# Windowed attention and a gated feed-forward block: another load order and transposition for one group of tokens, and some of its work on ScalarE

## The chip, the cores and the metric

The kernel runs on one core of one Trainium2 chip. The metric is the device time of the program in microseconds (us), median of several runs. Four engines compute: TensorE (PE: matmuls, and transposes written as matmuls against an identity; PEld is its weight load), VectorE (DVE), ScalarE (ACT) and GpSimd (POOL). POOL and SyncE (SP) here issue transfers, which sixteen DMA engines carry out. Matmuls write to PSUM, eight banks that the program uses in turn; an engine has to copy ("evict") what is needed from there to the on-chip memory.

## The reference

Attention over a window of 128 tokens plus four "sink" tokens at the start, and then a gated feed-forward block on the joined heads:

```python
batch, n_heads, seq, head_dim = (4, 8, 768, 64)      # n_sink, window = (4, 128)
scores = scale * np.matmul(q, k.transpose(0, 1, 3, 2))
keep = is_sink | in_window
scores = np.where(keep, scores, -1000000000.0)
a = np.exp(scores - np.max(scores, axis=-1, keepdims=True))
a = a / (np.sum(a, axis=-1, keepdims=True) + 1e-09)
attn = np.matmul(a, v)
x = attn.transpose(0, 2, 1, 3).reshape(B * S, H * D)   # 3072 tokens x 512
g = x @ w_gate                                         # 512 x 1536
out = (g * (1.0 / (1.0 + np.exp(-g))) * (x @ w_val)) @ w_out
```

## The kernel before

The 3072 tokens are cut into twelve groups of 256, three to a batch. For each group, queries and keys are brought into a form with the head dimension on the partitions (`qT`, `kT`), scores are computed (`step_S`), exponentials taken, values summed and normalised (`step_PV`), and the result is transposed (`step_X`) into `xT`, the input of the feed-forward block. That block works through `gate` units (two projections, tanh, two passes on VectorE) and `down` units (the output weights). All engines' programs are written in one fixed order: `weave` runs the units one after another and puts attention steps of later groups into them by slot number, so that TensorE always has something to do.

Groups get their transposed queries and keys in three ways: group 0 from a special load; groups 1 and 2 from a load in *row order* (four tokens of a head to a partition, 1 KB runs in memory), followed by small matmuls; groups 3 to 11 from a load in *token order* (one token to a partition, all heads, 256-byte runs), followed by DMA transposes.

```python
rowp = pool("rowp", 3); natp = pool("natp", 2)      # buffers: three and two
...
def load_rows(g, pairs=ALL, tensors=(0, 1)):        # row order, four DMAs
    ...
            nc.gpsimd.dma_start(x[64 * w:64 * (w + 1), i, pairs],
                                by_rows((k, q)[i], b, w, pairs, c * 256))

def load_nat(g):                                    # token order, four DMAs
    x = natp.tile([P, 2, 2, DM], BF16, tag="nat", name="nat")
    for i, src in ((0, k), (1, q)):
        for j in range(2):
            ...
            nc.gpsimd.dma_start(x[:, i, j].rearrange("p (h d) -> p h d", d=D),
                                src[b, :, t0:t0 + P].rearrange("h p d -> p h d"))
...
# order of the loads on GpSimd's queue
load_rows(1); load_v(0); load_gate(0); load_gate(1, (0,)); load_v(1)
load_gate(1, (1,)); load_gate(2)
...
load_rows(2); load_gate(3); load_v(2); load_gate(4); load_gate(5)
for i in range(4):
    load_out(i)
...                                                 # the prologue's compute
load_nat(3); load_v(3)

def step_T(g, i, p2, evict=None):                   # from row order: 16 matmuls of 64 x 64
    pt = bank([P, 2, 256], FP32, "pt")
    for pp in range(2):
        for r in range(4):
            for w in range(2):
                h = slice(64 * w, 64 * (w + 1))
                nc.tensor.matmul(pt[h, pp, r:256:4], x[h, i, p, r * D:(r + 1) * D],
                                 ident[h, h], start=True, stop=True, ...)
    # one eviction: keys on ScalarE, queries on VectorE

def xbar(g):                                        # from token order: four DMA transposes
    for j in range(2):
        for i in range(2):
            nc.sync.dma_start_transpose((kTs, qTs)[i][b][:, :, t0:t0 + P], nats[g][:, i, j])

def step_PV(g, j, hh, norm="v"):                    # one half of the heads of 128 tokens
    ...                                             # matmuls into po
    def dve():
        nc.vector.reciprocal(rcp, po[:, :, D:D + 1])
        if norm == "a":                             # four scalings on ScalarE
            for hq in range(4):
                nc.scalar.activation(xn[:, hq], po[:, hq, 0:D], AF.Copy, scale=rcp[:, hq])
        else:                                       # one multiply on VectorE
            nc.vector.tensor_tensor(xn, po[:, :, 0:D], rcp.broadcast_to([P, 4, D]), op=ALU.mult)
    if norm == "a":
        dve()                                       # written at once
    else:
        later.append(dve)                           # written behind the unit's own passes

def step_X(g, j, evict="v"):                        # groups 0, 1, 2, 4: four transposes on TensorE
    ...                                             # others: a DMA transpose
    # "a": copy on ScalarE at once; "now": on VectorE at once; "v": on VectorE later

weave(us, slots(                                    # units 0-11 and 12-17: gates; 18-23: down
    (0, [K(1)]), (1, PVs(1)[:2] + [A(step_PV, 1, 0, 1, "a"), A(step_PV, 1, 1, 1, "a"), flush]),
    (2, [A(step_X, 1, 0, "a"), A(step_X, 1, 1, "a")]),
    ((4, 4, 5, 5), T(2)), ((6, 7), Ss(2)), (6, [K(2)]),
    ((8, 8, 9, 9), PVs(2)),
    ((10, 11), [A(step_X, 2, 0, "now"), A(step_X, 2, 1, "now")]),
    (11, [L(A(load_nat, 4), A(load_v, 4))]),
    (12, [A(xbar, 3)]), (12, [L(A(load_nat, 5), A(load_v, 5))]),
    (15, [A(xbar, 4)]), (15, [L(A(load_nat, 6), A(load_v, 6))]),
    ((17, 18), Ss(3)), ...
    ((19, 19, 19, 20), PVs(3)), (20, Xs(3)),
    ((19, 20), Ss(4)), (19, [K(4)]), ...
```

Of the kernel before, what the change touches and what calls it, by code (L numbers as in the profile page):

```python
# [7 lines left out]
FP32 = mybir.dt.float32  # L8
BF16 = mybir.dt.bfloat16
# [5 lines left out]
def kernel(  # L15
# [12 lines left out]
    nc = tc.nc  # L28
    P = 128
# [3 lines left out]
    DM = moe_w_gate.shape[0]  # L33
# [5 lines left out]
    NP2 = H // 2  # L39
    GC = S // 256  # L40
# [12 lines left out]
    def pool(name, bufs, psum=False):  # L53
        if psum:
            return ctx.enter_context(
                tc.tile_pool(name=name, bufs=bufs, space=bass.MemoryType.PSUM))
        return ctx.enter_context(tc.tile_pool(name=name, bufs=bufs))

    const = pool("const", 1)
    wpool = pool("wpool", 1)  # L60
    rowp = pool("rowp", 3)
    natp = pool("natp", 2)
# [15 lines left out]
    def bank(shape, dtype, name):  # L78
        return psum.tile(shape, dtype, tag="b", name=name)


    rows, nats, vas = {}, {}, {}

    def by_rows(src, b, w, pairs, t0):

        hs = slice(2 * pairs.start + w, 2 * pairs.stop, 2)
        return src[b, hs, t0:t0 + 256].rearrange("p (m r) d -> m p (r d)", r=4)

    ALL = slice(0, NP2)

    def new_rows(g):
        rows[g] = rowp.tile([P, 2, NP2, 4 * D], BF16, tag="rows", name="rows")
        return rows[g]

    def load_rows(g, pairs=ALL, tensors=(0, 1)):
        b, c = divmod(g, GC)
        x = rows[g] if g in rows else new_rows(g)
        for i in tensors:
            for w in range(2):
                nc.gpsimd.dma_start(  # L100
                    x[64 * w:64 * (w + 1), i, pairs],
                    by_rows((k, q)[i], b, w, pairs, c * 256))

    def load_nat(g):
        b, c = divmod(g, GC)
        x = natp.tile([P, 2, 2, DM], BF16, tag="nat", name="nat")
        for i, src in ((0, k), (1, q)):
            for j in range(2):
                t0 = c * 256 + j * P
                nc.gpsimd.dma_start(  # L110
                    x[:, i, j].rearrange("p (h d) -> p h d", d=D),
                    src[b, :, t0:t0 + P].rearrange("h p d -> p h d"))
        nats[g] = x

    def load_v(g):
        b, c = divmod(g, GC)
        va = vpool.tile([P, 2, H, VS], BF16, tag=f"va{g}", name="va")
        nc.vector.memset(va[:, :, :, D:D + 1], 1.0)
        for j in range(2):
            t0 = c * 256 + j * P  # L120
            nc.gpsimd.dma_start(  # L121
                va[:, j, :, 0:D], v[b, :, t0:t0 + P].rearrange("h p d -> p h d"))
        vas[g] = va
# [3 lines left out]
    def load_gate(i, which=(0, 1)):  # L127
        f0, n = sum(FCH[:i]) * P, FCH[i] * P
        both = (wgs, moe_w_gate, "wg"), (wvs, moe_w_val, "wv")
        for lst, w, nm in (both[x] for x in which):  # L130
            t = wpool.tile([P, DMC, n], BF16, tag=f"{nm}{i}", name=nm)
            nc.gpsimd.dma_start(  # L132
                t, w[:, f0:f0 + n].rearrange("(c p) f -> p c f", p=P))
            lst.append(t)

    def load_out(i):
        n = DFC // 4
        t = wpool.tile([P, n, DM], BF16, tag=f"wo{i}", name="wo")
        nc.gpsimd.dma_start(
            t, moe_w_out[i * n * P:(i + 1) * n * P].rearrange("(c p) f -> p c f", p=P))  # L140
        wos.append(t)

    ident = const.tile([P, P], BF16)
# [6 lines left out]
    th8 = const.tile([P, 4, 4], FP32)  # L150
    lt8 = const.tile([P, 4, 4], FP32)
    sk = const.tile([P, 1], FP32)
    zero = const.tile([P, 512], BF16)
    one = const.tile([P, 1], FP32)
    warmed = const.tile([P, 1], FP32)
    KW = 32
    kss = const.tile([P, B, NP2, KW + 2 * NS], BF16)
    vsbs = []

    nc.vector.memset(one, 1.0)  # L160
    nc.vector.memset(zero, 0.0)
    nc.vector.memset(vcf, 0.0)
    nc.vector.memset(vcf[:, :, D:D + 1], 1.0)
    nc.vector.memset(kss, 0.0)
# [22 lines left out]
    for i in range(2):  # L187
        nc.gpsimd.dma_start(x0[:, i, 4:8], by_two((k, q)[i], 4))  # L188
    load_rows(1)
    load_v(0)  # L190
    load_gate(0)
# [2 lines left out]
    load_gate(1, (1,))  # L194
    load_gate(2)
    nc.gpsimd.tensor_copy(out=vcf[64:128], in_=vcf[0:64])
    load_rows(2)
    load_gate(3)
    load_v(2)
    load_gate(4)  # L200
    load_gate(5)
    for i in range(4):
        load_out(i)

# [14 lines left out]
    kTs, qTs, es_t, e_t, xns, xTs = {}, {}, {}, {}, {}, {}  # L219
    later = []  # L220

    def flush():
        for f in later:
            f()
        later.clear()

    def new_T(b):
        if b not in kTs:
            kTs[b] = kqtp.tile([P, NP2, S], BF16, tag="kT", name="kT")
            qTs[b] = kqtp.tile([P, NP2, S], BF16, tag="qT", name="qT")  # L230

    def step_T(g, i, p2, evict=None):
        b, c = divmod(g, GC)
        new_T(b)
        x = rows[g]
        pt = bank([P, 2, 256], FP32, "pt")
        for pp in range(2):
            p = 2 * p2 + pp
# [3 lines that stand above are left out]
                    nc.tensor.matmul(  # L242
                        pt[h, pp, r:256:4], x[h, i, p, r * D:(r + 1) * D],
                        ident[h, h], start=True, stop=True, skip_group_check=True)
        dst = (kTs, qTs)[i][b][:, 2 * p2:2 * p2 + 2, c * 256:(c + 1) * 256]
        if (evict or ("a", "v")[i]) == "a":
            nc.scalar.copy(out=dst, in_=pt)
        else:
            nc.vector.tensor_copy(out=dst, in_=pt)

    def xbar(g):
        b, c = divmod(g, GC)
        new_T(b)
        for j in range(2):
            for i in range(2):
                t0 = c * 256 + j * P
                nc.sync.dma_start_transpose(  # L257
                    (kTs, qTs)[i][b][:, :, t0:t0 + P], nats[g][:, i, j])
# [210 lines left out]
    def A(fn, *a):  # L469
        return lambda: fn(*a)  # L470

    def T(g):
        return [A(step_T, g, i, p2) for p2 in range(2) for i in range(2)]

    def Ss(g):
        return [A(step_S, g, p2) for p2 in range(2)]

    def PVs(g):
        return [A(step_PV, g, j, hh) for hh in range(2) for j in range(2)]
# [4 lines left out]
    def K(g):  # L484
        return A(step_K, g)
# [18 lines left out]
        return sl  # L504


    def fill(n, ps, cols=512):
        for _ in range(n):
            nc.tensor.matmul(ps[:, 0:cols], zero[:, 0:P], zero[:, 0:cols], start=True,
                             stop=True, skip_group_check=True)  # L510
# [23 lines left out]
    def pair_S(p, n=0):  # L534
        if p == 0:
            e_t[0] = epool.tile([P, H, 512], BF16, tag="e", name="e")
        pss = [bank([P, 512], FP32, "s") for _ in range(2)]
        fill(n, pss[0], 256)
        for kk, n, col in ((0, 256, P), (P, P, 3 * P)):
            for h in range(2):  # L540
                r = slice(h * D, (h + 1) * D)
                nc.tensor.matmul(
                    pss[h][:, col:col + n], kTs[0][r, p, kk:kk + P],
                    qTs[0][r, p, kk:kk + n], start=True, stop=True)
        for h in range(2):
            nc.scalar.activation(
                e_t[0][:, 2 * p + h, P:512], pss[h][:, P:512], AF.Exp, scale=scale)

    def pair_mask(p):
        e = e_t[0][:, 2 * p:2 * p + 2, P:512]  # L550
        m = mask0.rearrange("q (o a) x -> q o (a x)", o=1)[:, :, P:512]
        nc.vector.tensor_tensor(e, e, m.broadcast_to([P, 2, 384]), op=ALU.mult)

    fill(8, bank([P, 512], FP32, "w"))
    for i, p in ((0, 0), (1, 0), (0, 1), (1, 1)):
        cast(i, p)
    pair_T(0)
    pair_T(1)
    pair_S(0, 1)
    pair_S(1)  # L560
    pair_T(2)
    pair_T(3)
# [3 lines left out]
    for p in range(1, NP2):  # L566
        pair_mask(p)
    step_T(1, 0, 0, "a")
    step_T(1, 0, 1, "a")
    step_T(1, 1, 0, "a")  # L570
    step_T(1, 1, 1, "a")
# [12 lines left out]
    step_S(1, 1)  # L584
    later[:0] = masks1
    flush()
    load_nat(3)
    load_v(3)

    g0, g1, g2 = gates(0), gates(1), gates(2)  # L590
    us = [g0[0], g0[1], g0[2], g1[0], g1[1],
# [3 lines left out]
    def L(*fs):  # L595
        def f():
            for x in fs:
                x()
        return f

    weave(us, slots(
        (0, [K(1)]), (1, PVs(1)[:2] + [A(step_PV, 1, 0, 1, "a"), A(step_PV, 1, 1, 1, "a"), flush]),
        (2, [A(step_X, 1, 0, "a"), A(step_X, 1, 1, "a")]),
        ((4, 4, 5, 5), T(2)), ((6, 7), Ss(2)), (6, [K(2)]),
        ((8, 8, 9, 9), PVs(2)),
        ((10, 11), [A(step_X, 2, 0, "now"), A(step_X, 2, 1, "now")]),
        (11, [L(A(load_nat, 4), A(load_v, 4))]),
        (12, [A(xbar, 3)]), (12, [L(A(load_nat, 5), A(load_v, 5))]),
        (15, [A(xbar, 4)]), (15, [L(A(load_nat, 6), A(load_v, 6))]),
        ((17, 18), Ss(3)), (18, [A(step_ks, 1)]), (18, [A(step_vsb, 1)]),  # L610
        (17, [A(xbar, 5)]), (17, [L(A(load_nat, 7), A(load_v, 7))]),
# [60 lines left out]
```

The softmax here doesn't subtract the row's maximum and nothing guards it: scores larger than these inputs give would overflow.

## Time and profile before

| | before |
|---|---|
| time, median of 3 runs | 242.69 us (242.56 to 242.87) |
| span of the profiled execution | 240.2 us |
| TensorE busy | 230.8 us, 96% |
| VectorE busy | 159.6 us, 66% |
| ScalarE busy | 110.6 us, 46% |
| read from and written to the chip's large memory | 28.34 MB, 6.29 MB |

The profile is of one execution. Its page gives each engine's busy time; the span in forty slices of 6 us, one digit each in tenths; the DMA queues (q0 is the one that GpSimd feeds; q1 carries what SyncE issues, DMA transposes and output stores); the chain of work that ended last; and groups of equal instructions. A timeline lists instructions in order of time with equal ones merged: start, length, engine, line, operation, output<-inputs, shape, count, and in brackets the idle time before and what ended it. Matmuls overlap in the pipeline, so a matmul's printed length is longer than the time for which it holds TensorE.

### The profile page before, as it was taken

The numbers are of one execution on the slowest core, as the hardware profiler recorded it, in microseconds if no ns is written. First come the engines' busy times: TensorE is split into PE (matmuls) and PEld (weight loads), VectorE is DVE, ScalarE is ACT, GpSimd is POOL, SyncE is SP. The second block draws the span as 40 slices with busy tenths as digits, with TensorE's granted clock in tenths as the row PEclk, the third lists the DMA queues.
The fourth block names the chain that finished last, engine by engine and source line by source line (L and its number), as shares of the span: only waits on it lengthen the run. The fifth ranks groups of instructions, "written<-read, shape, count | busy, mean of one in ns | idle before, by whom it ended". The sixth has DMA issues, their size and how long they took to land.

```text
span 240.2 us, 5002 instructions
## 1 busy us (share of the span) xinstructions
PE 230.8 (96%) x1951; PEld 131.9 (55%) x1975; DVE 159.6 (66%) x340; ACT 110.6 (46%) x223; POOL 72.1 (30%) x94
## 2 busy tenths in 40 slices
PE   7999999997999999999999999999999999999994
PEld 3667877884545444454445444445444445488443
DVE  5698589886653698970597981488971498877000
ACT  4896474235541755511756612556611662232112
POOL 8976764705926209700082600000000000000000
PEclk9999999999999999999999999999999999999999
DMA  7999999999999999995699957550207200200132
GB/s 132 165 185 196 184 201 199 157 132 157 144 136 244 216 163 127 145 84 167 91 147 118 141 36 134 131 131 4 44 0 134 87 0 3 44 0 3 46 129 87
DMA packets 106694, 27.88 MB, mean 116 GB/s; under 512 B 92720, under 2 KB 103728, under 8 KB 106672
## 3 DMA queue, kind: packets, MB, share of 16 engines
q0 software_dynamic: 73568, 13.90, 75.1%
q1 hardware_dynamic: 32576, 13.41, 28.2%
q8 instruction: 15, 0.25, 0.4%
q10 hardware_dynamic: 528, 0.26, 0.4%
q14 instruction: 7, 0.06, 0.1%
HBM read 28.34 MB, written 6.29 MB: 144 GB/s over the span
## 4 chain that ended last, share of the span: by engine, by line
PE 72%; DMA 18%; POOL 3%; issue 2%; DVE 1%; SPq 1%; ACT 1%; POOLq 0%; DVEq 0%
PE pd L452 26%; PE pv L421 20%; PE pg L421 19%; DMA wv<-in_moe_w_val_dram 6%; DMA nat<-in_q_dram 5%; DMA rows<-in_k_dram 4%; DMA qT<-nat 4%; PE s L290 3%; PE o L353 3%; SPq L257 1%; POOL rows L100 1%; POOL va L121 1%; POOL x L188 1%; PE o L333 1%; PE pk L318 0%
## 5 line engine op out<-in xcount | busy, mean ns | idle before, releaser
L428 ACT ACTIVATE th<-pg 128x512 f32<-128x512 f32 x72 | 43.3, 602 | 68.2 <-PE pg L421 64.3
L421 PE MATMUL pv<-xT,wv 128*128 128x256 bf16 (+1 forms) x376 | 73.6, 325 | 0.7 <-DVE xn L367 0.2
L421 PE MATMUL pg<-xT,wg 128*128 128x256 bf16 (+1 forms) x377 | 73.5, 325 | 0.9 <-ACT xT L394 0.3
L434 DVE SCALAR_TENSOR_TENSOR u<-th,pg 128x512 bf16<-128x512 f32 x72 | 49.2, 683 | 34.0 <-ACT th L428 34.0
L452 PE MATMUL pd<-wo,ht 128*128 128x512 bf16 (+1 forms) x291 | 65.2, 370 | 0.6 <-issue 0.2
L435 DVE TENSOR_TENSOR ht<-u,pv 128x512 bf16<-128x512 bf16 x72 | 49.5, 688 | 12.2 <-PE pv L421 5.8
L421 PEld LDWEIGHTS <-wg 128*128 128x128 bf16 x384 | 37.4, 98 | 26.3 <-issue 1.2
L421 PEld LDWEIGHTS <-wv 128*128 128x128 bf16 x384 | 34.3, 98 | 19.9 <-issue 1.7
L297 ACT ACTIVATE e<-s 128x512 bf16<-128x512 f32 (+1 forms) x88 | 42.7, 580 | 4.9 <-PE s L290 4.9
L452 PEld LDWEIGHTS <-ht 128*128 128x128 bf16 x300 | 28.0, 98 | 28.5 <-issue 0.5
L456 ACT ACTIVATE ot<-pd 128x512 f32<-128x512 f32 (+1 forms) x25 | 14.6, 583 | 48.4 <-PE pd L452 46.4
L110 POOL DMA_DIRECT2D nat<-in_k_dram x18 | 15.9, 896 | 55.1 <-DMA qT<-nat 51.7
L302 DVE TENSOR_TENSOR e<-e,mask 128x1024 bf16<-128x1024 bf16 (+1 forms) x44 | 26.9, 649 | 4.0 <-ACT e L297 4.0
L121 POOL DMA_DIRECT2D va<-in_v_dram x24 | 21.6, 930 | 3.6 <-DMA wo<-in_moe_w_out_dram 2.1
L367 DVE TENSOR_TENSOR xn<-o,rcp 128x256 bf16<-128x256 f32 x46 | 19.5, 424 | 1.6
L353 PEld LDWEIGHTS <-e 128*128 128x128 bf16 x352 | 15.5, 98 | 8.2
L353 PE MATMUL o<-va,e 128*128 128x65 bf16 x352 | 17.4, 193 | 0.1
L110 POOL DMA_DIRECT2D nat<-in_q_dram x18 | 16.0, 911 | 0.5 <-DMA wv<-in_moe_w_val_dram 0.3
L290 PE MATMUL s<-qT,kT 64*128 64x128 bf16 (+1 forms) x240 | 13.1, 237 | 1.3 <-DMA qT<-nat 1.3
L290 PEld LDWEIGHTS <-kT 64*128 64x128 bf16 x240 | 7.7, 94 | 8.6 <-issue 7.6
L361 DVE RECIPROCAL rcp<-o 128x4 f32<-128x4 f32 x48 | 8.3, 176 | 5.5 <-PE o L353 5.4
L132 POOL DMA_DIRECT2D wv<-in_moe_w_val_dram x6 | 4.8, 807 | 1.0 <-DMA wv<-in_moe_w_val_dram 0.6
(62 smaller groups left out, 79.5 us busy)
## 6 DMA issues: line engine op xcount, KB each, us to landing
out_dram<-ot SPq DMA_DIRECT2D x23, 256.0 KB
va<-in_v_dram POOLq DMA_DIRECT2D x24, 128.0 KB, 6.7
nat<-in_k_dram POOLq DMA_DIRECT2D x18, 128.0 KB, 5.8
nat<-in_q_dram POOLq DMA_DIRECT2D x18, 128.0 KB, 6.6
wg<-in_moe_w_gate_dram POOLq DMA_DIRECT2D x6, 256.0 KB, 7.8
wv<-in_moe_w_val_dram POOLq DMA_DIRECT2D x6, 256.0 KB, 8.2
wo<-in_moe_w_out_dram POOLq DMA_DIRECT2D x4, 384.0 KB, 10.6
rows<-in_k_dram POOLq DMA_DIRECT2D x4, 128.0 KB, 6.9
```

The source lines that it names most:

```text
L110: nc.gpsimd.dma_start(x[:, i, j].rearrange("p (h d) -> p h d", d=D), src[b, :, t0:t0 + P].rearrange("h p d -> p h d"))
L121: nc.gpsimd.dma_start(va[:, j, :, 0:D], v[b, :, t0:t0 + P].rearrange("h p d -> p h d"))
L290: nc.tensor.matmul(pss[2 * pp + h][:, col:col + n], kTs[b][r, p, kk:kk + P], qTs[b][r, p, qq:qq + n], start=True, stop=True)
L297: nc.scalar.activation(e_t[g][:, h0 + h, lo:512], pss[2 * pp + h][:, lo:512], AF.Exp, scale=scale)
L302: nc.vector.tensor_tensor(e, e, m[:, :, lo:512].broadcast_to([P, 2, 512 - lo]), op=ALU.mult)
L353: nc.tensor.matmul(o, l, r, start=(c == 0 and i == 0), stop=(i == len(mms) - 1), skip_group_check=True)
L367: nc.vector.tensor_tensor(xn, po[:, :, 0:D], rcp.broadcast_to([P, 4, D]), op=ALU.mult)
L421: nc.tensor.matmul(ps[:, i * n:(i + 1) * n], ws[fi][:, c, fo * P:(fo + 1) * P], x[:, c], start=(c == 0), stop=(c == DMC - 1))
L428: nc.scalar.activation(th, pg, AF.Tanh, scale=0.5)
L434: nc.vector.scalar_tensor_tensor(u, th, 1.0, pg, op0=ALU.add, op1=ALU.mult)
L435: nc.vector.tensor_tensor(hts[tb][:, f:f + two].rearrange("p a n -> p (a n)"), u, pv, op=ALU.mult)
L452: nc.tensor.matmul(po, hts[tb][:, f, ts * P:(ts + 1) * P], wos[f // n][:, f % n, lo:hi], start=(f == 0), stop=(f == DFC - 1))
```

## The change

Group 2 is loaded in token order like the later groups, into the buffer of the row loads, and transposed by sixteen full 128 × 128 transposes on TensorE (`step_TN`) instead of sixty-four matmuls of 64 × 64; their PSUM tiles are bf16. Group 3's load moves ahead of the output weights, and its DMA transposes are written six units earlier (unit 6 instead of 12). For group 2, the second half of the heads is normalised on ScalarE, and both evictions of its transposed result are done there. The warm-up matmuls on zeros become narrower and more (17 of 256 columns for 8 of 512) and the zeros are written first. The change is for giving TensorE fewer and fuller transposes, relieving VectorE, and having group 3 ready sooner.

```diff
     def load_nat(g):
         b, c = divmod(g, GC)
-        x = natp.tile([P, 2, 2, DM], BF16, tag="nat", name="nat")
+        x = (natp if g > 2 else rowp).tile(
+            [P, 2, 2, DM], BF16, tag="nat" if g > 2 else "rows", name="nat")
...
-    zero = const.tile([P, 512], BF16)
+    zero = const.tile([P, 256], BF16)
...
+    nc.vector.memset(zero, 0.0)
     nc.vector.memset(one, 1.0)
-    nc.vector.memset(zero, 0.0)
...
-    load_rows(2)
+    load_nat(2)
     load_gate(3)
     load_v(2)
     load_gate(4)
     load_gate(5)
+    load_nat(3)
+    load_v(3)
     for i in range(4):
         load_out(i)
...
+    def step_TN(g, i, j):
+
+        b, c = divmod(g, GC)
+        new_T(b)
+        pt = bank([P, NP2, P], BF16, "pn")
+        for p in range(NP2):
+            nc.tensor.transpose(pt[:, p], nats[g][:, i, j, p * P:(p + 1) * P], ident)
+        t0 = c * 256 + j * P
+        if i == 0:
+            nc.scalar.copy(out=kTs[b][:, :, t0:t0 + P], in_=pt)
+        else:
+            nc.vector.tensor_copy(out=qTs[b][:, :, t0:t0 + P], in_=pt)
...
-    fill(8, bank([P, 512], FP32, "w"))
+    fill(17, bank([P, 512], FP32, "w"))
...
-    load_nat(3)
-    load_v(3)
...
-        ((4, 4, 5, 5), T(2)), ((6, 7), Ss(2)), (6, [K(2)]),
-        ((8, 8, 9, 9), PVs(2)),
-        ((10, 11), [A(step_X, 2, 0, "now"), A(step_X, 2, 1, "now")]),
+        ((4, 4, 5, 5), TN(2)), ((6, 7), Ss(2)), (6, [K(2)]),
+        ((8, 8), PVs(2)[:2]), (9, [A(step_PV, 2, 0, 1, "a"), A(step_PV, 2, 1, 1, "a")]),
+        ((10, 11), [A(step_X, 2, 0, "a"), A(step_X, 2, 1, "a")]),
         (11, [L(A(load_nat, 4), A(load_v, 4))]),
-        (12, [A(xbar, 3)]), (12, [L(A(load_nat, 5), A(load_v, 5))]),
+        (6, [A(xbar, 3)]), (12, [L(A(load_nat, 5), A(load_v, 5))]),
```

More of the change, by code (lines that the diff above doesn't have):

```diff
@@ L93, in new_rows, with load_rows @@
         return rows[g]
-    def load_rows(g, pairs=ALL, tensors=(0, 1)):
+    def load_rows(g):
         b, c = divmod(g, GC)
-        x = rows[g] if g in rows else new_rows(g)
-        for i in tensors:
+        x = new_rows(g)
+        for i in range(2):
             for w in range(2):
                 nc.gpsimd.dma_start(
-                    x[64 * w:64 * (w + 1), i, pairs],
-                    by_rows((k, q)[i], b, w, pairs, c * 256))
+                    x[64 * w:64 * (w + 1), i],
+                    by_rows((k, q)[i], b, w, ALL, c * 256))
     def load_nat(g):
         b, c = divmod(g, GC)
-        x = natp.tile([P, 2, 2, DM], BF16, tag="nat", name="nat")
+        x = (natp if g > 2 else rowp).tile(
+            [P, 2, 2, DM], BF16, tag="nat" if g > 2 else "rows", name="nat")
         for i, src in ((0, k), (1, q)):
@@ L470, in A, with TN @@
         return lambda: fn(*a)
-    def T(g):
-        return [A(step_T, g, i, p2) for p2 in range(2) for i in range(2)]
+    def TN(g):
+        return [A(step_TN, g, i, j) for j in range(2) for i in range(2)]
     def Ss(g):
@@ L504, in slots, with fill @@
         return sl
-    def fill(n, ps, cols=512):
+    def fill(n, ps, cols=256):
         for _ in range(n):
@@ L537, in pair_S @@
         pss = [bank([P, 512], FP32, "s") for _ in range(2)]
-        fill(n, pss[0], 256)
+        fill(n, pss[0])
         for kk, n, col in ((0, 256, P), (P, P, 3 * P)):
```

## The prediction

> **What bounds the kernel now.** I read the page first, then TensorE's timeline, then the chain of work and the DMA issues. Its first two parts:
>
> ```profile
> PE 230.8 (96%) x1951; PEld 131.9 (55%) x1975; DVE 159.6 (66%) x340; ACT 110.6 (46%) x223; POOL 72.1 (30%) x94
> ...
> PE   7999999997999999999999999999999999999994
> ...
> DMA  7999999999999999995699957550207200200132
> ...
> q0 software_dynamic: 73568, 13.90, 75.1%
> ```
>
> TensorE has work almost everywhere, so only less work for it, or a shorter hole in it, moves the end. The DMA engines are full for eighteen of forty slices (about 108 us), so any hole closed before that must also find its data there. Matmul durations overlap; what a matmul costs is the distance to the next start. So I read starts, on TensorE's timeline (start, us, instruction, count, idle before and who ended it). Group 2's transposes:
>
> ```profile
> 25.01 1.04 PE L421 MATMUL pg<-xT,wg 128*128 128x256 bf16 x8
> 25.97 1.08 PE L242 MATMUL pt<-ident,rows 64*64 64x64 bf16 x32
> 26.99 1.05 PE L421 MATMUL pv<-xT,wv 128*128 128x256 bf16 x8
> ```
>
> Thirty-two small matmuls hold TensorE 26.99 − 25.97 = 1.02 us; the second 32 take 1.01 us (28.84 to 29.85). Then the two holes:
>
> ```profile
> 41.43 0.28 PE L391 MATMUL px<-ident,xn 128*128 128x128 bf16 x2
> 42.53 0.28 PE L391 MATMUL px<-ident,xn 128*128 128x128 bf16 x2 [0.82 <-DVE xn L367]
> ...
> 44.40 0.39 PE L391 MATMUL px<-ident,xn 128*128 128x128 bf16 x4
> 44.62 1.04 PE L421 MATMUL pv<-xT,wv 128*128 128x256 bf16 x8
> ...
> 54.23 1.04 PE L421 MATMUL pg<-xT,wg 128*128 128x256 bf16 x8
> 56.53 0.51 PE L290 MATMUL s<-qT,kT 64*128 64x256 bf16 x8 [1.26 <-DMA qT<-nat]
> ```
>
> Four full transposes take 44.62 − 44.40 = 0.22 us, 55 ns each. The first hole is 42.53 − 41.43 − 2 × 0.055 = 0.99 us, waiting for the second half of group 2's normalised rows. A gate's eight matmuls take 0.87 us, so the second hole is 56.53 − 54.23 − 0.87 = 1.43 us, waiting for group 3's transposed queries. Over the rest of the kernel I find no start gap above 0.5 us once the prologue (15 us) is past. The chain through the second hole:
>
> ```profile
> 24.14 8.28 DMA wv<-in_moe_w_val_dram
> ...
> 33.57 11.56 DMA nat<-in_q_dram
> ...
> 45.15 1.19 SPq L257
> ...
> 47.76 8.63 DMA qT<-nat
> ...
> 56.53 0.51 PE s L290 x8
> ```
>
> Group 3's queries were issued behind four pieces of output weights and landed at 46.0 us; their four DMA transposes were issued at 43.2 to 47.8 and the last landed about 56.4.
>
> **What the skill says.** "TensorE: Matmul & The Clock Gate", back-to-back issue gap: N/2.4 + 2.5 ns warm, and a floor near 25 ns for small N. That is 56 ns for 128 columns and 29 ns for 64; the trace has 55 ns and 1.02/32 = 32 ns (switching included), so it agrees: a 64 × 64 transpose wastes most of the array. "VectorE: DVE Perf Modes", why PSUM operands drop a tier: a copy from PSUM reaches 2× at most, and 1× for fp32. The trace agrees: 128x512 from PSUM took 692 ns as fp32 (qT) and 422 ns as bf16 (xT). "DMA: Bandwidth & Descriptors", why small descriptors are slow: short runs pay a fixed cost each. Here a 128 KB transfer in row order (512-byte packets) landed 0.77 us after the one before it on average, in token order (128-byte packets) 0.93 us: it agrees, mildly. The same page's queues section: a DMA engine goes round-robin between its queues. In the trace group 3's DMA transposes took about 2.2 us each while loads were queued, and group 4's last two about 0.6 us each once the loads had run dry at 57.8 us.
>
> **The change part by part.**
>
> *Transposes.* 64 matmuls (2.03 us) become 16 at 55 ns = 0.88 us, in the same two slots: −1.15 us on TensorE. The query eviction falls from 692 to 422 ns on VectorE, off the path.
>
> *Load of group 2.* Row order landed at 22.5 to 25.0 us. Four token-order transfers at 0.93 us behind the same 21.83 us (last piece of value weights ahead) land at 22.8, 23.7, 24.6, 25.6. The slot at 25.97 now needs the first and third, the second slot the others: no wait. All later loads slip 4 × (0.93 − 0.77) = 0.6 us; gate piece 3 then lands at 26.8 for a need near 29.6.
>
> *Normalisation on ScalarE.* VectorE is 10.66 of 12 us busy between 32 and 44 us and runs late. Before, the second half stood behind a whole gate: the gate's two passes (1.37 us), then reciprocal and multiply twice. Now the two reciprocals stand ahead of these passes, at about 40.5 and 40.7 in the old clock, and ScalarE scales in eight instructions, 1.75 us for eight earlier in the trace. The first four are done near 41.7 against a need at 41.54: hole 0.25 instead of 0.99, −0.74 us.
>
> *Evictions on ScalarE.* The second now stands behind that gate's tanh: matmuls of the gate 0.87, tanh to about +1.67, copy 0.59, so ready near +2.25 where the next gate wants it at 0.87 + 0.22 + 0.87 = +1.96. New hole 0.3 us; group 1's evictions, done so already, cost 0.33 us at 23.26.
>
> *Group 3 early.* Behind gate piece 5 (34.5 + 0.6) its six transfers at 0.93 land at 36.0 to 40.6. Its DMA transposes start at 36 instead of 43.2 and compete with output weights instead of group 4's loads. The first took over 4 us before and the others 2.2; allowing 3 each against larger packets, they end at 46 to 51. The scores want them at 55.1 − 1.15 − 0.74 + 0.3 = 53.5: hidden, −1.43 us. The output weights end near 52 and are wanted from 54.9 (the last quarter near 57): hidden.
>
> *Warm-up.* 17 × 256 columns for 8 × 512, on a shorter memset placed first: 0.15 us earlier in, 6% more columns. The first real transposes follow the casts at 4.7 us anyway: zero.
>
> Sum: −1.15 − 0.74 + 0.3 − 1.43 = −3.0 us, which would be 239.7.
>
> **What may take it back.** The loads themselves are not faster. Group 4's last load landed at 54.88 after everything ahead of it, group 3's transposes included; that sum grows by 0.6, so about 55.5. Its own transposes were issued at 49.2 to 55.0 and done about 59.5, for scores starting at 63.3: 3.8 us of room. Now the scores want them at 60.3. They are issued in turn as the loads land, about 53, 54.6, 55.9, 57.2 with 1.25 us each in the queue. And they lose the quiet stretch: before, group 5's load could not start until group 3's buffer was free (issued at 56.95 after a 9.37 us wait); now the buffer is free near 50 and group 5 queues directly behind group 4. At 1 to 2.2 us each the last is done between 60.5 and 62.5. So a new hole of 0 to 2.5 us before group 4's scores; I take 1.1. If it stays away, the same shortage shows at group 3's output transposes, done about 77 for gates at 78.05. I take 1.1 once for both: 242.69 − 3.0 + 1.1 = 240.8.
>
> **Rivals.** (1) Pure TensorE account: every hole closes, 239.7. For it: TensorE is the 96% engine and the DMA groups later have slack (group 6's transposes are done some 3 us before need). Against it: the full DMA row above. (2) DMA pace sets everything up to 78 us: new waits eat 2 to 3 us, 242 to 242.8. For it: the DMA share is 2.1 in the windows 44 to 58 and 58 to 66 us, the highest I see; against: 3.8 us of room at group 4 and a total of loads only 0.6 us larger. (3) ScalarE becomes late: between 39 and 45 us it gains eight scalings and two copies, 1.75 + 1.2 us, on 6.67 busy of 12. A delay of tanh only delays VectorE, which loses 1.7 us there; I allow 0.5 us, 241.3.
>
> **Range and chances.** The parts that are plain counting give −1.15; the two holes −1.9 more with their new small one; the shortage gives back 0 to 3. So 239.3 to 242.6 around 240.8. 2% is 4.9 us: below 237.8 is more than all I can find, 0.02. Above 247.5 needs a load of group 2 or a gate piece several us late, 0.03.
>
> **What would show it.** Right: sixteen transposes in 0.9 us; group 2's hole under 0.4; no hole before group 3's scores; a hole of about 0.3 at the first gate of the third block, released by ScalarE's xT; and a wait for group 4's DMA transposes of up to 2.5 us. Wrong: a wait for group 2's load, or for group 3's transposes beyond 53 us (output weights' packets starve them); group 4's scores without any wait and 239.7 or less (loads drain better than I count); or a hole later than 90 us.

## The result, and the profile after

The changed kernel takes 246.17 us (median of 4 runs, 245.3 to 246.7) against 242.78 us (4 runs, 242.56 to 243.09): a ratio of 1.0135, 95% interval 1.0101 to 1.0169. It is slower, and outside the predicted range of 239.3 to 242.6.

The page of the changed kernel: engine shares, then 40 slices of 6.1 us, then the queue that GpSimd feeds.

```profile
PE 231.0 (95%) x1912; PEld 132.9 (55%) x1936; DVE 158.0 (65%) x336; ACT 113.0 (46%) x233; POOL 73.2 (30%) x94
...
PE   7998999999299999999999999999999999999994
...
PEclk9999999999889999999999999999999999999999
DMA  7999999999999999994499993651204200200132
...
q0 software_dynamic: 76640, 13.90, 78.0%
```

One digit of TensorE's row tells most: slice eleven (61 to 67 us) is busy for two tenths. And the granted clock falls in that slice and the next; in the profile before its row is nines throughout. Slice ten, where the hole before group 3's scores was, has gone from seven tenths to nine, and slice four has lost a tenth. The DMA row is full until slice eighteen, as before.

TensorE's timeline shows that the parts meant for it work:

```profile
26.44 0.61 PE L260 MATMUL pn<-ident,nat 128*128 128x128 bf16 x8
26.88 1.04 PE L437 MATMUL pv<-xT,wv 128*128 128x256 bf16 x8
...
40.65 0.43 PE L407 MATMUL px<-ident,xn 128*128 128x128 bf16 x4
40.92 1.04 PE L437 MATMUL pv<-xT,wv 128*128 128x256 bf16 x8
...
53.75 0.50 PE L306 MATMUL s<-qT,kT 64*128 64x256 bf16 x8
```

Eight full transposes hold TensorE for 0.44 us. The hole in group 2's output transposes is gone (0.27 us from start to start for four, 0.05 over their own 0.22). Group 3's scores follow their gate without a wait. Then, on the same timeline:

```profile
59.98 0.59 PE L468 MATMUL pd<-wo,ht 128*128 128x512 bf16 x2
61.88 0.23 PE L306 MATMUL s<-qT,kT 64*128 64x128 bf16 x2 [1.30 <-DMA qT<-nat]
65.36 0.93 PE L306 MATMUL s<-qT,kT 64*128 64x256 bf16 x10 [3.26 <-DMA qT<-nat]
66.63 0.63 PE L468 MATMUL pd<-wo,ht 128*128 128x512 bf16 x1 [0.33 <-issue]
...
70.67 0.62 PE L306 MATMUL s<-qT,kT 64*128 64x128 bf16 x12
```

The two halves of group 4's scores on the timeline of the kernel before:

```profile
63.29 0.62 PE L290 MATMUL s<-qT,kT 64*128 64x128 bf16 x12
...
67.33 0.61 PE L290 MATMUL s<-qT,kT 64*128 64x128 bf16 x12
```

A 512-column matmul holds TensorE for 0.216 us. So it could have begun group 4's scores at 59.98 + 2 × 0.216 = 60.41 us; before, they began at 63.29. So 2.88 us had been won by then. Two holes follow: 61.88 − 60.41 = 1.47, and 65.36 − 61.88 − 2 × 0.027 = 3.43 us (0.027 is one of the small score matmuls), 4.9 together. The line at 66.63 shows a second cost: a 512-column matmul is printed with 0.63 us instead of 0.38. The windows of the same kernel (busy time by engine, then granted clock, DMA share, GB/s) show why:

```profile
60.00:65.00 5.00, 0.81 (x9) 0.19 (x6) 1.14 (x5) 0.00 (x0) 0.00 (x0) 1.00 1.95 155
65.00:68.40 3.40, 2.70 (x22) 1.10 (x23) 1.12 (x2) 2.24 (x5) 2.47 (x3) 0.50 1.54 197
68.40:75.00 6.60, 6.55 (x63) 3.28 (x63) 3.12 (x9) 3.15 (x6) 6.60 (x9) 1.00 1.85 176
```

From 65.0 us on TensorE had half its clock for 3.4 us. The second half of group 4's scores starts at 70.67 us against 67.33 before, 3.34 late, of which 4.9 − 2.88 = 2.02 is the hole less the gain; so the half clock cost 1.3. The distance then stays: 96.29 against 92.93 us at the next small hole that both have. The sum −2.88 + 4.9 + 1.3 = +3.3 is the difference of the spans, 243.5 − 240.2. (The 1.3 is what is left over here; the run with the hole filled, below, measures it by itself.) Three of the four timed runs have a mean clock of 0.985 instead of the profiled 0.991, which fits a second such stretch (a run below with 0.985 has 6.8 us at half clock in its trace); those are the runs at 245.85 to 246.7.

The chain into the hole:

```profile
40.36 14.48 DMA nat<-in_q_dram
...
58.01 7.31 DMA qT<-nat
65.32 0.04 issue
65.36 0.93 PE s L306 x10
```

Group 4's queries landed at 54.8 and 55.7 us; the last of its DMA transposes was issued at 58.01 and landed 7.3 us later.

### The profile page after: what moved, and what is told of

It is laid out like the page before. It is cut to its first block, busy times and chain, and to the rows that moved or that the text cites. A ratio compares the mean times of both kernels' runs of the same rounds, so it can differ in the third digit from the quotient of the medians.

```text
span 243.5 us, 4930 instructions
## 1 busy us (share of the span) xinstructions
PE 231.0 (95%) x1912; PEld 132.9 (55%) x1936; DVE 158.0 (65%) x336; ACT 113.0 (46%) x233; POOL 73.2 (30%) x94
## 4 chain that ended last, share of the span: by engine, by line
PE 69%; DMA 17%; POOL 7%; issue 2%; SPq 1%; DVE 1%; ACT 1%; POOLq 0%; DVEq 0%
PE pd L468 24%; PE pv L437 19%; PE pg L437 18%; DMA wv<-in_moe_w_val_dram 8%; DMA nat<-in_q_dram 6%; PE s L306 3%; PE o L369 3%; DMA qT<-nat 3%; POOL va L122 2%; POOL wg L133 1%; SPq L273 1%; POOL rows L100 1%; POOL wo L140 1%; POOL wv L133 1%; POOL nat L111 1%
## 5 line engine op out<-in xcount | busy, mean ns | idle before, releaser
L468 PE MATMUL pd<-wo,ht 128*128 128x512 bf16 (+1 forms) x291 | 65.9, 373 | 0.8 <-issue 0.3
L111 POOL DMA_DIRECT2D nat<-in_k_dram x20 | 17.7, 893 | 57.2 <-DMA qT<-nat 56.5
L383 DVE TENSOR_TENSOR xn<-o,rcp 128x256 bf16<-128x256 f32 x44 | 18.7, 424 | 1.5
L306 PE MATMUL s<-qT,kT 64*128 64x128 bf16 (+1 forms) x240 | 13.8, 242 | 4.6 <-DMA qT<-nat 4.6
L111 POOL DMA_DIRECT2D nat<-in_q_dram x20 | 17.8, 907 | 0.7 <-DMA wg<-in_moe_w_gate_dram 0.7
```

Of the source, the lines that this page charges most:

```text
L306: nc.tensor.matmul(pss[2 * pp + h][:, col:col + n], kTs[b][r, p, kk:kk + P], qTs[b][r, p, qq:qq + n], start=True, stop=True)
L468: nc.tensor.matmul(po, hts[tb][:, f, ts * P:(ts + 1) * P], wos[f // n][:, f % n, lo:hi], start=(f == 0), stop=(f == DFC - 1))
```

## The experiments

By the packets in the trace (512 to a transpose), group 4's four DMA transposes run from 56.1 to 64.7 us, one after another. Their packets take 2.1, 1.7, 1.8 and 1.6 us; behind the first and the second stand pauses of 0.85 and 0.6 us in which only loads move. GpSimd issues group 5's load when group 3's buffer comes free. First its timeline before, then after the change:

```profile
56.95 1.75 POOL L110 DMA_DIRECT2D nat<-in_k_dram  x2 [9.37 <-DMA qT<-nat]
```

```profile
53.69 1.75 POOL L111 DMA_DIRECT2D nat<-in_k_dram  x2 [6.68 <-DMA qT<-nat]
```

The theory (A) was that these loads share the DMA engines with group 4's transposes and slow them. The rivals: group 4's own loads land late (B); the DMA engines are behind with everything (D); and for the clock, that only the hole's length counts.

**Holding group 5's load, first try.** One more buffer of the pool was claimed, unused, ahead of group 5's:

```diff
+        if g == 5:
+            natp.tile([P, 2, 2, DM], BF16, tag="nat", name="nat")
```

> The kernel after, with one edit: group 5's load takes the buffer of group 4 instead of that of group 3, so it cannot start before group 4's DMA transposes are done. Nothing is left out of the computation. Theory A (group 4's transposes are slow because group 5's loads, freed early, share the DMA engines with them): they end near 60 us instead of 65, the hole of 4.9 us before group 4's scores shrinks to under 0.6 us, no half-clock stretch follows, and the time is 239.8 to 240.8 us, faster than both kernels. Theory B (the hole is there because group 4's own loads land late behind the output weights and the whole of the load work): the hole stays over 3 us and the time over 243 us.

Measured: 246.74 us, ratio 1.0174 (1.0125 to 1.0223). The edit did not act: GpSimd issues the load at 53.34 us. It says nothing of A or B. In effect it is a second profile of the changed kernel, with holes of 2.07 and 3.13 us at the same place and 6.8 us at half clock.

**Filling the hole.**

```diff
         pss = [bank([P, 512], FP32, "s") for _ in range(4)]
+        if g == 4 and p2 == 0:
+            fill(40, pss[0])
```

> The kernel after, with 40 matmuls of 256 columns on zeros (about 4.4 us) written just ahead of group 4's first scores; their output is overwritten, the result is unchanged. The hole is filled with them and its end is set by the DMA transposes as before. Theory A (a hole of some 5 us costs more than its length, because TensorE's clock is halved for one or two stretches of 3.4 us after it): the clock stays whole, mean over 0.99, and the time is 1.3 to 2.7 us below the kernel after, 243.4 to 244.9 us. Theory B (only the length of the hole counts; the lower mean clock is a label): 245.5 to 246.7 us, as the kernel after.

Measured: 244.71 us, ratio 1.0071 (1.005 to 1.0092). Its timeline:

```profile
60.07 4.53 PE L527 MATMUL s<-zero 128*128 128x256 bf16 x40
64.53 0.23 PE L308 MATMUL s<-qT,kT 64*128 64x128 bf16 x2
65.62 0.56 PE L308 MATMUL s<-qT,kT 64*128 64x256 bf16 x10 [0.86 <-DMA qT<-nat]
```

The scores start as late as in the changed kernel (65.62 against 65.36), but the clock stays whole (mean 0.998), and the kernel is 1.5 us faster than the unfilled one; the intervals of the two ratios do not overlap. So the half clock is a cost of its own, and idling is what brings it.

**The order of the loads alone,** in the kernel before:

```diff
     load_gate(5)
+    load_nat(3)
+    load_v(3)
     for i in range(4):
         load_out(i)
...
     flush()
-    load_nat(3)
-    load_v(3)
```

> The kernel before, with one edit: group 3's query, key and value loads stand ahead of the output weights. Group 2's load, transposes, normalisation and evictions, and the warm-up are as before. Theory A (this move alone makes the loss: it frees group 3's buffer early and lets group 5's loads run into group 4's transposes): no hole before group 3's scores, a hole of 2 to 4 us before group 4's, followed by a half-clock stretch; 244.3 to 246.3 us. Theory B (the loss comes from the other parts, which bring TensorE to group 4's scores earlier or load group 2 in small packets): at most 242.2 us.

**The change without that order,** group 3's loads back behind the output weights:

```diff
-    load_nat(3)
-    load_v(3)
     for i in range(4):
         load_out(i)
+    load_nat(3)
+    load_v(3)
```

> The kernel after, with group 3's loads put back behind the output weights; the other parts of the change stay. Theory A (until some 65 us the DMA engines set the pace, so TensorE's 1.6 us saved on group 2 are lost again in the next wait for data): the hole before group 3's scores grows from 1.4 to 3 to 4 us and the time is 242.5 to 244.5 us, depending on whether a half-clock stretch follows. Theory B (what is saved on TensorE stays saved, since group 3's data had little more to do): 240.7 to 241.6 us.

Measured: 245.78 us, ratio 1.013 (1.0089 to 1.017), with the order alone; 245.27 us, ratio 1.0106 (1.007 to 1.0143), without it. First the timeline with the order alone, then the one without it:

```profile
62.76 0.23 PE L292 MATMUL s<-qT,kT 64*128 64x128 bf16 x2
66.38 0.93 PE L292 MATMUL s<-qT,kT 64*128 64x256 bf16 x10 [3.39 <-DMA qT<-nat]
```

```profile
52.45 1.04 PE L437 MATMUL pg<-xT,wg 128*128 128x256 bf16 x8
57.50 0.83 PE L306 MATMUL s<-qT,kT 64*128 64x256 bf16 x8 [4.01 <-DMA qT<-nat]
```

With the order alone the hole stands before group 4's scores (66.38 − 62.76 − 2 × 0.027 = 3.6 us); without it, before group 3's, grown from 1.43 to 57.50 − 52.45 − 0.87 = 4.2 us. Each is followed by a half-clock stretch. So neither half of the change alone is the culprit: each gives TensorE time that it then spends waiting for DMA transposes. Without the order these are also later themselves: group 3's scores start at 57.50 us against 56.53 in the kernel before. The second figure lies above its range: I had the hole at 3 to 4 us and let the half clock be uncertain.

**Holding group 5's load, second try.** The two buffers get names, and group 5 takes group 4's:

```diff
-    natp = pool("natp", 2)
+    natp = pool("natp", 1)
...
-            [P, 2, 2, DM], BF16, tag="nat" if g > 2 else "rows", name="nat")
+            [P, 2, 2, DM], BF16, tag=f"nat{g % 2 if g > 4 else g - 3}" if g > 2 else "rows", name="nat")
```

> The kernel after, with the two token-order buffers named, so that group 5 takes that of group 4 and cannot start to load before group 4's DMA transposes are done; nothing else differs and nothing is left out. (An earlier edit for the same purpose left group 5's load where it was, issued at 53.3 us.) Theory A (group 5's loads, freed early, slow group 4's transposes): group 5's load is issued near 60 us, the transposes end near 60 us, the hole before group 4's scores is under 1 us instead of 4.9, no half-clock stretch; 239.8 to 241.0 us. Theory B (the hole is there because group 4's own loads land late, behind the output weights): the hole stays over 3 us and the time over 243.5 us.

Measured: 249.47 us, ratio 1.0256 (1.0202 to 1.0309). The load was held (issued at 61.97 us), and TensorE's timeline has this:

```profile
60.48 0.23 PE L306 MATMUL s<-qT,kT 64*128 64x128 bf16 x2
60.94 0.56 PE L306 MATMUL s<-qT,kT 64*128 64x256 bf16 x10 [0.23 <-DMA qT<-nat]
...
73.70 2.11 PE L468 MATMUL pd<-wo,ht 128*128 128x512 bf16 x9
82.67 1.86 PE L437 MATMUL pg<-xT,wg 128*128 128x512 bf16 x4 [6.87 <-DMA xT<-xn]
```

On the hole, A is right and B falls: group 4's loads landed as late as ever (53.3 to 57.0 us), but the last three transposes took 0.7, 0.7 and 0.8 us instead of 1.7, 1.8 and 1.6, all four ran from 56.2 to 60.5 us, 4.3 instead of 8.6, and the hole is 0.4 us. On the time A was wrong, and B's "over 243.5" is met without its hole: 7.0 us of waiting reappear (82.67 − 73.70 − 9 × 0.216), before the gates that use group 3's output transposes. SyncE's timeline of that kernel:

```profile
65.32 1.52 SPq L273 DMA_TRANSPOSE kT<-nat  x1
...
71.15 1.38 SPq L273 DMA_TRANSPOSE qT<-nat  x1
72.62 1.06 SPq L473 DMA_DIRECT2D out_dram<-ot  x2
73.79 2.65 SPq L402 DMA_TRANSPOSE xT<-xn  x2
```

SyncE issues in program order. Group 3's output transposes stand behind group 5's, and these now wait for the held load.

**Group 4's load ahead of half the output weights,** not held; and **both edits.**

```diff
-    for i in range(4):
+    for i in range(2):
+        load_out(i)
+    load_nat(4)
+    for i in range(2, 4):
         load_out(i)
...
-        (11, [L(A(load_nat, 4), A(load_v, 4))]),
+        (11, [A(load_v, 4)]),
```

> The kernel after, with group 4's query and key load moved ahead of the last two of the four pieces of output weights (4.8 us earlier by their landings); group 5's load is not held. Theory A: group 4's transposes then run against output weights and values, before group 5's loads arrive, and end at 58 to 60.5 us: hole under 1 us, 239.8 to 241.6 us. Theory B: the same from another cause, so this run alone does not tell the two apart; with the held run it does. Rival C (the DMA engines are simply full until 65 us, and whatever is moved ahead makes something else late): a hole moves to the first matmuls on the late output weights, near 57 us, and the time stays over 243.5 us.

> Both edits together: group 5's load held behind group 4's transposes, and group 4's load ahead of the last two pieces of output weights. Theory A: no hole before group 4's scores, the whole 2.9 us counted for TensorE is kept: 239.4 to 240.3 us, faster than both kernels. Rival C: a hole of over 2 us near 57 us or at the output transposes of group 3 near 76 us, and over 242 us.

Measured: 243.93 us, ratio 1.0039 (0.9963 to 1.0116), unclear against the kernel before, for the first; 249.09 us, ratio 1.024 (1.0187 to 1.0293), for both. In the first, group 4's transposes were issued from 48.5 us on, but the first moved only from 52.5 to 56.5 us and the others took 1.6, 1.6 and 2.1 us against output weights and values; the hole shrank to 2.4 us, not under 1. The late weights made none, so the hole that rival C names is not there, though the median lies in its "over 243.5". Both edits together have the held kernel's hole: 7.4 us before the same gates.

**The warm-up alone,** in the kernel before (the three lines of the change on the zeros and the fill).

> The kernel before with the warm-up of the changed kernel alone (17 matmuls of 256 columns for 8 of 512, zeros written first). Theory A (the first real transposes follow the first casts, so the warm-up is worth nothing): 242.2 to 242.9 us, and the clock becomes full at 7.0 us as before. Rival (the narrower warm-up lets the clock drop or ends late): over 243.5 us.

Measured: 242.75 us, ratio 0.9978 (0.9925 to 1.003). It is worth nothing that can be measured.

**Output transposes first,** in the held kernel: group 5's transposes, and the load behind them, go after group 3's output transposes.

```diff
-        (17, [A(xbar, 5)]), (17, [L(A(load_nat, 7), A(load_v, 7))]),
-        ((19, 19, 19, 20), PVs(3)), (20, Xs(3)),
+        ((19, 19, 19, 20), PVs(3)), (20, Xs(3)),
+        (20, [A(xbar, 5)]), (20, [L(A(load_nat, 7), A(load_v, 7))]),
```

> The kernel with group 5's load held behind group 4's DMA transposes (which had no hole before group 4's scores, but one of 7 us before the gates that use group 3's output transposes), with one more edit: group 5's DMA transposes stand behind group 3's output transposes in SyncE's order instead of ahead of them, and the load that reuses group 5's buffer goes with them. Theory E (the 7 us hole came from the order on SyncE's queue: the output transposes stood behind transposes that waited for the held load): the hole near 77 us goes, and a hole of 0 to 3 us appears before group 5's scores, whose transposes now end near 78 us; 240 to 243.5 us. Theory D (too much DMA work altogether): a hole of over 4 us stays in the stretch 75 to 82 us; over 245 us.

Measured: 245.12 us, ratio 1.0098 (1.0069 to 1.0127).

```profile
77.06 0.23 PE L306 MATMUL s<-qT,kT 64*128 64x128 bf16 x2 [0.80 <-DMA qT<-nat]
79.54 0.93 PE L306 MATMUL s<-qT,kT 64*128 64x256 bf16 x10 [2.25 <-DMA qT<-nat]
```

The 7 us hole is gone, so it was SyncE's order (E). Holes of 0.97 and 2.42 us stand before group 5's scores instead, with a half-clock stretch, and the time is above E's range. In kind this is E; in size it leans towards D: a load that is held makes the next group late.

**Group 4 transposed on TensorE,** so that it needs no DMA transposes at all:

```diff
-        (15, [A(xbar, 4)]), (15, [L(A(load_nat, 6), A(load_v, 6))]),
         ((17, 18), Ss(3)), (18, [A(step_ks, 1)]), (18, [A(step_vsb, 1)]),
-        (17, [A(xbar, 5)]), (17, [L(A(load_nat, 7), A(load_v, 7))]),
+        (18, TN(4)), (18, [L(A(load_nat, 6), A(load_v, 6))]),
+        (18, [A(xbar, 5)]), (18, [L(A(load_nat, 7), A(load_v, 7))]),
```

> The kernel after, with group 4's four DMA transposes replaced by sixteen transposes on TensorE (as group 2 has them), in unit 18 behind group 3's scores; the loads that reuse group 4's buffer and the next DMA transposes are written behind them. The computation is whole. Theory A (the loss is only the wait for group 4's DMA transposes, which crawl while loads are queued; its data are on the chip by 56 us): no hole before group 4's scores and no half-clock stretch, 0.9 us more on TensorE; 240.2 to 241.4 us, faster than both kernels. Theory D (the DMA engines are behind with everything, and the next user of them takes the hole over): a hole of over 2 us before group 3's output transposes are used (near 77 us) or before group 5's scores, and over 243 us.

Measured: 240.05 us (239.85 to 241.46), ratio to the kernel before 0.9877 (0.9844 to 0.9911). It beats both kernels. Its page and timeline:

```profile
PEclk9999999999999999999999999999999999999999
```

```profile
56.05 0.39 PE L260 MATMUL pn<-ident,nat 128*128 128x128 bf16 x4
56.27 0.38 PE L468 MATMUL pd<-wo,ht 128*128 128x512 bf16 x1
...
60.45 0.38 PE L468 MATMUL pd<-wo,ht 128*128 128x512 bf16 x1
60.98 0.61 PE L306 MATMUL s<-qT,kT 64*128 64x128 bf16 x12
```

Sixteen transposes at 0.22 us for four cost 0.9 us; group 4's scores start at 60.98 without a wait for data, although its loads land no earlier (53.1 to 55.5 us) and group 5's load is not held.

**The same without the group 2 parts:** the kernel before with the new order and group 4 on TensorE, run beside the full one.

> The kernel before, with group 3's loads ahead of the output weights and group 4 transposed on TensorE, and nothing else of the change: group 2 stays in row order with its small transposes and VectorE's normalisation and evictions. Theory A (the group 2 parts are worth what was counted for them, 1.15 + 0.74 - 0.3 = 1.6 us, wherever no wait for data follows): 1.2 to 2.0 us slower than the kernel with all parts and group 4 on TensorE, 241.2 to 242.1 us. Theory F (the group 2 parts are worth nothing even then, and the gain comes from the order and group 4 alone): within 0.5 us of that kernel, 239.7 to 240.6 us.

> The kernel after with group 4 transposed on TensorE once more, on the same chip as its neighbour for the comparison: 239.7 to 240.6 us.

Measured: 242.37 us, ratio 0.9978 (0.9967 to 0.9989), and 240.25 us, ratio 0.9888 (0.9871 to 0.9905). So with no wait for data behind them the group 2 parts are worth 2.1 us, a little more than the 1.2 to 2.0 expected; F falls. (The pair differs in the warm-up too, which alone was worth nothing.) In the two profiles group 4's scores start at 62.92 and 60.79 us. About 0.3 of that 2.1 is the first real transposes starting at 5.08 and 4.78 us, when the first load lands, which differs from one profile to another (4.75 and 5.08 in the kernels before and after).

## Why the prediction was wrong

**Transposes: right.** Counted 0.88 us for sixteen; measured 0.44 + 0.45.

**Load of group 2: right, with a wait not foreseen.** It landed at 23.8 to 25.8 us (said: 22.8 to 25.6) and nothing waited for it. The last piece of value weights ahead of it landed at 22.9 instead of 21.8, and TensorE waited 0.6 us for it. A wait of 0.3 us stands there in the warm-up run too, where group 2 is in row order; whether token order makes it longer stays open.

**Normalisation and evictions on ScalarE: right.** The hole fell to 0.05 us (said: 0.25), and a gap of 0.29 us opened at the first gate of the third block (said: 0.3).

**Group 3 early: right in effect, wrong in its margin.** I had its transposes done at 46 to 51 us. The last landed at 53.1, for scores that began at 53.75: on time by half a us, which is luck and not the forecast.

**When TensorE would want group 4: right.** Said 60.3 us, measured 60.4.

**What may take it back: the step that failed.** The place, the cause and the order of events were as written, and group 4's last load landed at 55.7 (said: about 55.5). But the prediction has "At 1 to 2.2 us each the last is done between 60.5 and 62.5". With the last issued at about 57.2, that leaves 3.3 to 5.3 us from its issue to its landing. It was issued at 58.01 and landed at 65.3: 7.3 us. The packets of each took what had been allowed, 1.6 to 2.1 us. Left out was the waiting around them: 2.8 us from the first issue (53.26) to the first packet (56.08), the pauses of 0.85 and 0.6 us, and 0.6 us from the last packet to the landing. The profile before had shown it. The prediction's own line "47.76 8.63 DMA qT<-nat" says that group 3's last transpose landed 8.6 us after its issue with loads queued, and "the first took over 4 us" is there the time from issue to first packet (43.24 to 47.30), with 1.6 us of packets behind it. The nearest likeness was group 5 (issued from 60.62 on, landed at 73.46, the last 8.2 us after its issue), against group 5's and 6's loads; I did not use it. Only group 4, whose loads ran out, had taken as little as forecast: its last was issued at 55.04 and landed at 59.23. The term "a new hole of 0 to 2.5 us [...] I take 1.1" was 4.9.

**A missing term.** The sum had no entry for the clock. The Trainium skill's page "TensorE: Matmul & The Clock Gate", under "What's actually happening", says that the array's clock falls to half after an idle window of about 3.4 us; the prediction cites that page for other things. Here the clock did fall to half behind 4.9 us of holes, for 3.41 us, and that cost 1.3 us.

**The rivals.** Rival 2 (DMA pace sets everything up to 78 us) is right in that new waits ate the gain, and more than its 2 to 3 us. But the pace of the loads did not set everything: with group 4 on TensorE, group 4's loads land when they did, and the kernel takes 240.05 us. The held kernel also shows the second place named for the shortage, group 3's output transposes, though there it was the order on SyncE that brought it. Rival 3, a late ScalarE, did not appear beyond the gap of 0.29 us.

## What to carry to other kernels

Before filling a hole by moving a load forward, ask what the buffer that it frees lets start, and measure the next waiter's transfers where the queue stays full, not where it runs dry, and from issue to landing. A wait of a few us costs TensorE more than its length, since the clock drops behind it. Where DMA transposes queue behind loads and TensorE has a microsecond to spare, transposing there (0.9 us for 256 tokens) can be cheaper than another order of the transfers: here it turned a loss of 1.4% into a gain of 1.2%.

## What the runs showed of the hardware that was not expected

- A DMA transpose of 128 tokens by 512 took 0.6 to 0.8 us with the load queue empty (group 4's last two in the kernel before, its last three in the held kernel) and 1.6 to 2.1 us with it full (group 4 in the changed kernel), while the loads beside it kept landing every 0.8 to 1.9 us. Where both had packets to move, they shared evenly by number: from 62.0 to 62.75 us of the changed kernel 303 packets of the transposes and 311 of the loads. Alone, 988 packets of the transposes moved in one us (held kernel, 58 to 59 us).
- The half clock follows shorter holes than I would have thought: 3.41 us of it after one idle time of 2.2 us (group 4's load ahead of the weights), while 1.3 us of idle time in the kernel before brought none in its profile. (Six of the 73 timed runs of that kernel have a mean clock of 0.991 to 0.993 and took 244.4 to 245.2 us, as one such stretch would give; none of them was profiled.) The idle window of about 3.4 us cited above was not needed in full there; the measurement decides.
- Apart from one that starts as the kernel ends, the half-clock stretches are 3.41 us or twice that, and the full-clock time ahead of each is a multiple of the same length: 58.03 us (17 times) in the changed kernel, 61.44 (18 times) with the order alone, 75.09 (22 times) in the held kernel. So in these traces the clock changes on a fixed beat. The half clock began 0.4 us before the hole's end in the changed kernel (64.99 us) and 1.3 us after it with group 4's load ahead of the weights (63.84 us).
- The changed kernel's mean clocks of 0.991 and 0.985 fit one and two such stretches behind the same hole, which would be most of its spread from 245.3 to 246.7 us.
